# One state product for two chunks: 104-column chunks in the scan of a delta-rule attention kernel

## The chip, the cores and the metric

The kernel runs on one NeuronCore of one Trainium2 chip. The metric is the device time of one execution in microseconds (us); the time of a kernel is the median of several executions.

## The reference

What is computed first is a linear recurrence with a 40 x 40 state for each of 4 x 8 heads, over 768 steps; then a mixture of experts is applied to its output (8 experts, each token goes to one of them or is passed through).

```python
def _attn_ref(r, k, v, w, a, b):          # each [4, 8, 768, 40]
    state = zeros((B, H, D, D))
    for t in range(S):
        y[:, :, t] = einsum('bhd,bhde->bhe', rt, state)
        Sa = einsum('bhde,bhe->bhd', state, at)
        state = state * wt[:, :, None, :] - einsum('bhd,bhe->bhde', Sa, bt)
        state = state + einsum('bhd,bhe->bhde', vt, kt)
def reference(...): x = attn_out as [3072, 320]; return _moe_ref(x, w_skip, w_gate, w1, w2)
```

## The kernel before

**Chunks.** The 768 steps are cut into 24 chunks of 32 steps (`c`), and the 32 heads into two sides (`x` = 0, 1) of 16 heads (`u`). Two chunks make a pair, `c//2`: decays, masks and the inverse triangular matrices are made for a pair, and four chunks share one triangular inversion. For each side a tile `R1[x][c%2]`, 128 partitions x 16 heads x 72 columns, stands for a chunk. Its columns 0 to 39 are the transposed state with the decay of the pair; its columns 40 to 71 are one column for each of the 32 queries `r` of the chunk. Its partitions hold 40 rows of state, 32 rows of `v`, and 32 rows of solved terms `U`.

**The steps of one chunk and side**, with the engines and lines:

- `rs` (L288): 16 products of the state `SS[x]` with `r`, 32 columns each; two copies into columns 40 to 71 of the state rows. In an even chunk the copies are on VectorE and multiply by a decay `Dx` (L292), in an odd chunk they are plain ScalarE copies (L293).
- `m2` (L207, L209): 16 products of `v` and `r`, 32 columns; four ScalarE copies into the rows of `v`. It runs one chunk ahead.
- `ux` (L302, L304): 16 products of `R1` with the keys, 72 columns; one ScalarE copy into `UXs`.
- `uq` (L313, L315, L317): 16 products with the inverse triangle, 72 columns; four ScalarE copies into the `U` rows; a mask multiply over the 32 query columns on GpSimd.
- `sst` (L325, L330): the new state, twice. 16 products give it transposed (`ST`), copied into columns 0 to 39 of the next chunk's `R1` (L335 on ScalarE after an even chunk, L334 on VectorE with the decay of the next pair after an odd one); 16 more with the operands exchanged give it untransposed (`S2`), copied into `SS` (L338), which only `rs` reads.
- `yy` (L348, L352): 16 products of the query columns give the output.

Every matmul of these steps is fp32 and appears in the trace as two TensorE instructions, so that 16 products are a group of 32.

**The order of the work** is written out by hand for TensorE, ScalarE and VectorE: each issues in the order of the program text. One turn of the chunk loop runs `rs(c,0)`, `uq(c-1,1)`, `yy(c-1,0)`, `ux(c,0)`, `sst(c-1,1)`, `m2(c+1,0)`, `uq(c,0)`, `rs(c,1)`, `yy(c-1,1)`, `sst(c,0)`, `ux(c,1)`, `m2(c+1,1)`. Between them stand pieces of other work: `m1` (L163 to L174, products of the keys), `kbt` (L185, L188) and `wtt` (L197, L199), which are transposes; `route` (L628 to L684), which transposes the finished output, picks an expert and scatters tokens; scans of the decays (L114, L126); and the generator `T()`, one step of the triangular inversion on VectorE (L228, L230). GpSimd's order alone is set by a scheduler. With four chunks per inversion, a turn of the loop comes in four kinds, `j = c%4`: scans stand in the even turns (`j` = 0 and 2), transposes `kbt` in the odd ones.

**Loads.** `load_rv` brings `r` and `v` of a chunk as one tile (L104), issued from GpSimd's queue at the end of a turn, two chunks ahead into two buffers; its buffer is free when `rs` and `m2` of the older chunk are done.

After the loop come the experts (L729 to L797), some 150 us that read nothing of the above but the tokens.

Of the kernel before, what the change touches and what calls it, by code (L numbers as in the profile page):

```python
# [57 lines left out]
def attn(ctx,tc,i,m,out,X):  # L58
# [43 lines left out]
    def load_rv(c,E=G):  # L102
        if c>=NC: return
        rvt[c]=wk2.tile([128,2,16,32],F32,tag="rvt",name="rvt"); E.dma_start(rvt[c],i['rv'][c])  # L104
# [95 lines left out]
    def m2(c,x):  # L200
        if c>=NC: return
        t=rvt[c]; rr=t[:,0].rearrange("p (b h) t -> p b h t",b=2); vv=t[:,1].rearrange("p (b h) t -> p b h t",b=2)
        Pp=ps_p.tile([128,4,32],F32,tag="pp",name="psP")
        for hh in range(4):
            for b in (0,2,1,3):
                s=slice(64*(b//2),64*(b//2)+40)
                TE.matmul(Pp[32*b:32*b+32,hh,:],vv[s,b%2,2*hh+x,:],rr[s,b%2,2*hh+x,:],start=True,stop=True)  # L207
        for b in range(4):
            A.copy(R1[x][c%NR1][ao[x]:ao[x]+32,4*b:4*b+4,40:72],Pp[32*b:32*b+32])  # L209
# [70 lines left out]
    def rs(c,x):  # L280
        if c>=NC: return
        cc=c%2; rr=rvt[c][:,0].rearrange("p (b h) t -> p b h t",b=2)
        R=R1[x][c%NR1]; e=slice(eo[x],eo[x]+40)
        RS=ps_c.tile([128,8,32],F32,tag="pc",name="psRS")
        for hh in range(4):
            for b in (0,2,1,3):
                s=slice(64*(b//2),64*(b//2)+40); v=(b%2)*4+hh
                TE.matmul(RS[s,v,:],SS[x][:,b//2,v,:],rr[:,b%2,2*hh+x,:],start=True,stop=True)  # L288
        for bh in range(2):
            s=slice(64*bh,64*bh+40)  # L290
            o=R[e,8*bh:8*bh+8,40:72]
            if cc==0: V.tensor_tensor(o,RS[s],H[c//2]['Dx'][x][s].unsqueeze(2).broadcast_to([40,8,32]),ALU.mult)  # L292
            else: A.copy(o,RS[s])  # L293
    UXd={}
    def ux(c,x):
        if c>=NC: return
        R=R1[x][c%NR1]; l1=L1[x][(c//2)%NL]
        UX=ps_c.tile([128,4,72],F32,tag="pc",name="psUX")
        for hh in range(4):
            for b in range(4):  # L300
                u=4*b+hh
                TE.matmul(UX[32*b:32*b+32,hh,:],l1[:,u,c%2,:],R[:,u,:],start=True,stop=True)  # L302
        UXs=wk2.tile([128,4,72],F32,tag="UX",name="UXs")
        A.copy(UXs,UX)  # L304
        UXd[x]=UXs
    def uq(c,x):
        if c<0: return
        R=R1[x][c%NR1]; Tb=TBa[(c//2)%NTB]; uu=slice(uo[x],uo[x]+32)
        UQ=ps_c.tile([128,4,72],F32,tag="pc",name="psUQ")
        for hh in range(4):  # L310
            for b in range(4):
                q=slice(32*b,32*b+32)
                TE.matmul(UQ[q,hh,:],Tb[q,x*8+hh*2+c%2,:],UXd[x][q,hh,:],start=True,stop=True)  # L313
        for b in range(4):
            A.copy(R[uu,4*b:4*b+4,:],UQ[32*b:32*b+32,:,:])  # L315
# [1 line left out]
        (V if c==NC-1 else G).tensor_tensor(R[pq,:,40:72],R[pq,:,40:72],mQ[pq].unsqueeze(1).broadcast_to([64,16,32]),ALU.mult)  # L317
    def sst(c,x):
        if c<0 or c+1>=NC: return
        R=R1[x][c%NR1]; Rn=R1[x][(c+1)%NR1]; l2=L2[x][(c//2)%NL2]; cc=c%2; e=slice(eo[x],eo[x]+40)  # L320
        ST=ps_s.tile([128,8,40],F32,tag="ps",name="psST")
        for hh in range(4):
            for b in (0,2,1,3):
                u=4*b+hh; v=(b%2)*4+hh; s=slice(64*(b//2),64*(b//2)+40)
                TE.matmul(ST[s,v,:],l2[:,cc,u,:],R[:,u,0:40],start=True,stop=True)  # L325
        S2=ps_s.tile([128,8,40],F32,tag="ps",name="psS")
        for hh in range(4):
            for b in (0,2,1,3):
                u=4*b+hh; v=(b%2)*4+hh; s=slice(64*(b//2),64*(b//2)+40)
                TE.matmul(S2[s,v,:],R[:,u,0:40],l2[:,cc,u,:],start=True,stop=True)  # L330
        for bh in range(2):
            s=slice(64*bh,64*bh+40)
            o=Rn[e,8*bh:8*bh+8,0:40]
            if cc==1: V.tensor_tensor(o,ST[s],H[c//2+1]['Dx'][x][s].unsqueeze(2).broadcast_to([40,8,40]),ALU.mult)  # L334
# [5 lines left out]
    def yy(c,x):  # L340
# [4 lines left out]
        for hh in range(4):  # L345
            for b in range(4):
                u=4*b+hh
                TE.matmul(Y[32*b:32*b+32,2*hh+x,:],R[:,u,40:72],l2[:,cc,u,:],start=True,stop=True)  # L348
# [556 lines left out]
```

## Time and profile before

| | |
|---|---|
| median of 3 runs | 662.38 us (660.09 to 664.48) |
| the profiled execution's own time | 663.83 us |
| its span, first to last instruction | 662.1 us |
| loop over chunks, about | 66 us to 510 us |
| mean granted TensorE clock | 0.888 |
| VectorE / ScalarE / GpSimd busy | 489.7 / 419.5 / 324.2 us |

The rows that follow come from one profiled execution. A row of the groups gives line, engine, operation, tiles, shape and count, then busy time and mean duration of one, then the idle time before it. A row of the chain gives start, length and what ran: the chain follows the last instruction back to what released it, each time, or to its predecessor on its engine. A row of the timeline gives start, length, instructions merged into it, and in brackets the idle time ahead. "issue" in the place of a releaser is a wait for which the trace shows no cause. `PEld` is TensorE's weight load.

### The profile page before, as it was taken

What the parts mean: (1) busy time and instruction counts of PE and PEld (TensorE: products, weight loads), DVE (VectorE), ACT (ScalarE), POOL (GpSimd) and SP (SyncE); (2) the same over time, 40 slices, a digit from 0 to 9 for tenths busy, and PEclk for the clock granted to TensorE, in tenths of its full rate; (3) what the DMA queues carried; (4) which work ended last, traced back from release to release, by engine and by line L of the source; (5) the groups of instructions that cost most, each with busy time, mean ns of one, the idle gap of its engine ahead of it and who ended that gap; (6) DMA issues with size and microseconds to landing.
All of it is one profiled execution on the core that took longest, in us unless ns stands there. A gap on an engine that the chain in (4) does not pass through costs nothing.

```text
span 662.1 us, 33508 instructions
## 1 busy us (share of the span) xinstructions
PE 515.5 (78%) x14772; PEld 432.2 (65%) x14772; DVE 489.7 (74%) x1182; ACT 419.5 (63%) x1151; POOL 324.2 (49%) x246
## 2 busy tenths in 40 slices
PE   4777776676776787767785877878886899999995
PEld 1543456565664576656664666666775599999995
DVE  7998697858997479973999736864166457888881
ACT  5463674586965778567785677887885354555540
POOL 5481951648545375553946442223132155666661
PEclk8786895799977898878889689988788999999998
DMA  7473665352443525335253333453365266676210
GB/s 227 152 242 107 166 207 160 104 177 63 139 125 107 174 63 150 109 112 168 83 156 88 107 113 81 140 153 113 105 178 167 73 183 201 214 229 216 77 48 24
DMA packets 67446, 91.06 MB, mean 138 GB/s; under 512 B 32564, under 2 KB 54657, under 8 KB 65806
## 3 DMA queue, kind: packets, MB, share of 16 engines
q1 hardware_dynamic: 62350, 74.05, 38.1%
q0 software_dynamic: 4944, 14.80, 6.6%
q8 instruction: 118, 1.93, 1.2%
q14 instruction: 34, 0.28, 0.1%
HBM read 74.03 MB, written 17.08 MB: 138 GB/s over the span
## 4 chain that ended last, share of the span: by engine, by line
PE 24%; DVE 11%; ACT 8%; issue 5%; DMA 2%; POOL 1%; SPq 0%; POOLq 0%; DVEq 0%; ACTq 0%
PE pc L782 5%; PE ps L793 4%; PE px L782 3%; ACT R1t L315 2%; PE py L793 2%; ACT L2t L188 2%; DVE M L228 2%; PE ps L325 2%; DVE ti L789 2%; PE pc L313 1%; PE pc L288 1%; DVE M L230 1%; PE ps L330 1%; ACT SS L338 1%; ACT R1t L209 1%
## 5 line engine op out<-in xcount | busy, mean ns | idle before, releaser
L317 POOL TENSOR_TENSOR R1t<-R1t,mc 64x512 f32<-64x512 f32 x46 | 60.5, 1315 | 104.7 <-ACT R1t L315 72.6
L315 ACT COPY R1t<-pc 32x288 f32<-32x288 f32 x192 | 74.9, 390 | 20.7 <-PE pc L313 17.6
L730 POOL TENSOR_TENSOR WL<-WR,WH 128x1280 fp32r<-128x1280 f32 (+1 forms) x21 | 57.7, 2782 | 8.7 <-ACT WH L729 8.6
L188 ACT COPY L2t<-pq 64x160 f32<-64x160 f32 x184 | 52.8, 287 | 7.5 <-PE pq L185 5.1
L684 POOL DMA_INDIRECT xg<-XS,ix x24 | 25.5, 1064 | 64.3 <-DMA xg<-XS,ix 26.0
L325 PE MATMUL ps<-R1t,L2t 128*40 128x40 f32 x1472 | 48.2, 221 | 11.0 <-issue 5.3
L143 POOL TENSOR_TENSOR WR<-WR,M 128x1024 f32<-128x1024 f32 (+1 forms) x19 | 44.2, 2332 | 25.8 <-DVE M L114 19.7
L228 DVE TENSOR_TENSOR M<-M 128x22 f32<-128x22 f32 (+10 forms) x110 | 55.0, 500 | 0.0
L325 PEld LDWEIGHTS ps<-R1t,L2t 128*40 128x40 f32 x1472 | 39.3, 132 | 18.9 <-ACT R1t L315 8.9
L338 ACT COPY SS<-ps 40x320 f32<-40x320 f32 x92 | 38.7, 420 | 19.9 <-PE ps L330 18.5
L209 ACT COPY R1t<-pq 32x128 f32<-32x128 f32 x184 | 47.2, 256 | 5.5 <-PE pq L207 1.3
L288 PE MATMUL pc<-rvt,SS 128*40 128x32 f32 x1472 | 44.9, 216 | 7.2 <-issue 4.8
L288 PEld LDWEIGHTS pc<-rvt,SS 128*40 128x40 f32 x1472 | 38.3, 135 | 15.4 <-issue 7.8
L330 PE MATMUL ps<-L2t,R1t 128*40 128x40 f32 x1472 | 42.9, 218 | 6.5 <-issue 6.4
L313 PE MATMUL pc<-UXs,TB 32*32 32x72 f32 x1536 | 43.1, 255 | 6.0 <-issue 5.9
L330 PEld LDWEIGHTS ps<-L2t,R1t 128*40 128x40 f32 x1472 | 38.2, 134 | 7.3 <-issue 7.2
L230 DVE TENSOR_TENSOR M<-M 128x22 f32<-128x22 f32 (+10 forms) x110 | 40.8, 371 | 0.0
L230 DVE TENSOR_TENSOR px<-px,M 128x168 f32<-128x168 f32 (+8 forms) x150 | 39.1, 260 | 1.4
L729 ACT CAST WH<-WR 128x1024 fp32r<-128x1024 f32 (+1 forms) x35 | 39.6, 1132 | 0.0
L313 PEld LDWEIGHTS pc<-UXs,TB 32*32 32x32 f32 x1536 | 32.1, 122 | 11.4 <-issue 8.9
L789 DVE CAST ti<-xe 128x2 int32<-128x2 f32 x8 | 39.3, 4911 | 0.2
L174 DVE STREAM_TRANSPOSE M<-pq 128x128 f32<-128x128 f32 x40 | 12.1, 308 | 36.9 <-ACT M L165 24.3
(240 smaller groups left out, 1529.3 us busy)
## 6 DMA issues: line engine op xcount, KB each, us to landing
rvt<-rv POOLq DMA_DIRECT2D x21, 512.0 KB, 3.9
WR<-kb SPq DMA_DIRECT2D x10, 1024.0 KB
WR<-w SPq DMA_DIRECT2D x16, 640.0 KB
WR<-w SPq DMA_DIRECT2D x16, 512.0 KB
M<-wt SPq DMA_DIRECT2D x9, 520.5 KB
M<-at SPq DMA_DIRECT2D x8, 512.0 KB
WR<-w SPq DMA_DIRECT2D x16, 256.0 KB
R1t<-vt SPq DMA_DIRECT2D x48, 80.0 KB
```

Source lines behind the costliest of these rows:

```text
L188: A.copy(L2[x][h%NL2][64-64*x:128-64*x,c,bb*4:bb*4+4,:],pt[64*c:64*c+64,:,64*x:64*x+40])
L209: A.copy(R1[x][c%NR1][ao[x]:ao[x]+32,4*b:4*b+4,40:72],Pp[32*b:32*b+32])
L228: V.tensor_tensor(tv,NLt[:,j,j+1:32].unsqueeze(2).broadcast_to([128,n,k]),X[:,j,lo:hi].unsqueeze(1).broadcast_to([128,n,k]),ALU.mult)
L230: for tv,xv in q: V.tensor_tensor(xv,xv,tv,ALU.subtract)
L288: TE.matmul(RS[s,v,:],SS[x][:,b//2,v,:],rr[:,b%2,2*hh+x,:],start=True,stop=True)
L313: TE.matmul(UQ[q,hh,:],Tb[q,x*8+hh*2+c%2,:],UXd[x][q,hh,:],start=True,stop=True)
L315: A.copy(R[uu,4*b:4*b+4,:],UQ[32*b:32*b+32,:,:])
L317: (V if c==NC-1 else G).tensor_tensor(R[pq,:,40:72],R[pq,:,40:72],mQ[pq].unsqueeze(1).broadcast_to([64,16,32]),ALU.mult)
L325: TE.matmul(ST[s,v,:],l2[:,cc,u,:],R[:,u,0:40],start=True,stop=True)
L330: TE.matmul(S2[s,v,:],R[:,u,0:40],l2[:,cc,u,:],start=True,stop=True)
L730: def low(s,E,o,x,h): E.tensor_tensor(s.R(o),x,h,ALU.subtract)
L782: for n,(a,b) in enumerate(mm): TE.matmul(ph[:,g],R(a),R(b),start=n==0,stop=n==7)
```

## The change

An even chunk's `R1` gets 104 columns: 40 of state, 32 with the queries of the *next* (odd) chunk, 32 with its own. `rs` of an even chunk multiplies the state with both chunks' queries (64 columns), and `m2` and the steps after it carry the extra 32 columns along. `sst` of an even chunk then applies its keys to 72 columns at once: out come the transposed state and, beside it, that state times the odd chunk's queries, which are just the 72 columns that the odd chunk's `R1` needs. So an odd chunk has no `rs`, and an even chunk makes no `S2` and no copy into `SS`. The mask is needed for an even chunk's own 32 columns alone. `r` is laid out by pairs on the host (tile `rrt`, own columns second) and `v` by chunks (`vvt`); GpSimd issues a load of `vvt` in each turn and one of `rrt` in each odd turn.

```diff
+        rrt[h]=wk2.tile([128,16,64],F32,tag="rrt",name="rrt"); E.dma_start(rrt[h],i['rr'][h])
     def m2(c,x):
+        n=(64,32)[c%2]
-        Pp=ps_p.tile([128,4,32],F32,tag="pp",name="psP")
+        Pp=ps_p.tile([128,4,n],F32,tag="pp",name="psP")
...
     def rs(c,x):
-        if c>=NC: return
+        if c>=NC or c%2: return
-        RS=ps_c.tile([128,8,32],F32,tag="pc",name="psRS")
+        RS=ps_c.tile([128,8,64],F32,tag="pc",name="psRS")
...
-            if cc==0: V.tensor_tensor(o,RS[s],H[c//2]['Dx'][x][s].unsqueeze(2).broadcast_to([40,8,32]),ALU.mult)
-            else: A.copy(o,RS[s])
+            V.tensor_tensor(R[e,8*bh:8*bh+8,40:104],RS[s],H[c//2]['Dx'][x][s].unsqueeze(2).broadcast_to([40,8,64]),ALU.mult)
     def ux(c,x):
+        R=R1[x][c%NR1]; l1=L1[x][(c//2)%NL]; n=RW[c%2]
-        UX=ps_c.tile([128,4,72],F32,tag="pc",name="psUX")
+        UX=ps_c.tile([128,4,n],F32,tag="pc",name="psUX")
...
     def sst(c,x):
+        if cc==0:
+            for hh in range(4):
+                for b in (0,2,1,3):
+                    u=4*b+hh; s=slice(64*(b//2),64*(b//2)+40)
+                    TE.matmul(P2[s,b%2,72*hh:72*hh+72],l2[:,0,u,:],R[:,u,0:72],start=True,stop=True)
+            for bh in range(2):
+                A.copy(Rn[e,8*bh:8*bh+8,:].rearrange("p (b h) n -> p b (h n)",b=2),P2[64*bh:64*bh+40,:,0:288])
+            return
...
             load_rv(c+2,G if c else SP)
+            if c%2 or c==0: load_rr((c+3)//2,G if c else SP)
```

`RW` is (104, 72); `uq` takes its width from it in the same way.
`P2` joins the two PSUM banks that `ST` and `S2` used in turn.

The first place is ScalarE in an odd turn with `j` = 3, from the copies of `sst(c-1,1)` to those of `sst(c,0)`. Before:

```order
L335 COPY R1t<-ps_102 40x8x40 x2
L338 COPY SS_117<-ps_101 40x320 x2
L647 ACTIVATE ex<-sb 128x16
L209 COPY R1t<-pq_104 32x4x32 x4
L315 COPY R1t<-pc_99 32x288 x4
L293 COPY R1t<-pc_100 40x8x32 x2
L188 COPY L2t<-pq_105 64x160 x4
L232 COPY M<-px_106 128x32x8
L338 COPY SS_116<-ps_101 40x320 x2
```

The same stretch now, where all lines have moved down by some ten:

```order
L334 COPY R1t<-ps 40x576 x2
L661 ACTIVATE ex<-sb 128x16
L217 COPY R1t<-pq_102 32x4x64 x4
L322 COPY R1t<-pc_100 32x288 x4
L195 COPY L2t<-pq_103 64x160 x4
L240 COPY M<-px_104 128x32x8
L351 COPY SS_115<-ps 40x320 x2
```

The two copies into `SS` of the even chunk and the two of the odd chunk's `rs` are gone; the copies of `sst` grew from 320 to 576 elements per partition and those of `m2` from 128 to 256.

The second place is TensorE, in the same kind of turn, from its start. Before:

```order
L288 MATMUL pc_100<-rvt,SS_116 40x32 x16
L313 MATMUL pc_99<-UXs,TB 32x72 x16
L185 MATMUL pq_105<-mc,WR 128x104 x4
L348 MATMUL py_103<-L2t,R1t 32x40 x16
L636 MATMUL pq_104<-wg,xT 32x9 x12
L302 MATMUL pc_100<-R1t,L1t 32x72 x16
L185 MATMUL pq_105<-mc,WR 128x104 x4
L325 MATMUL ps_102<-R1t,L2t 40x40 x16
L330 MATMUL ps_101<-L2t,R1t 40x40 x16
```

And now:

```order
L320 MATMUL pc_100<-UXs,TB 32x104 x16
L192 MATMUL pq_103<-mc,WR 128x104 x4
L361 MATMUL py_101<-L2t,R1t 32x40 x16
L650 MATMUL pq_102<-wg,xT 32x9 x12
L309 MATMUL pc_99<-R1t,L1t 32x72 x16
L192 MATMUL pq_103<-mc,WR 128x104 x4
L332 MATMUL ps<-R1t,L2t 40x72 x16
```

The product with `r` at the head of the turn and the second state product are gone; `uq` of the even chunk's side 1 has 104 columns and its state product 72.

The third place is GpSimd, whose order the scheduler made anew, in an even turn with `j` = 2. Before:

```order
L684 DMA xg<-XS,ix 2048x322 x2
L170 TENSOR_TENSOR M<-M,mc 128x256
L143 TENSOR_TENSOR WR<-WR,M 128x32x32
L317 TENSOR_TENSOR R1t<-R1t,mc 64x16x32
L132 COPY D_3446<-D 40x8 x2
L132 COPY D_3449<-D 40x8 x2
L143 TENSOR_TENSOR WR<-WR,M 128x32x32
```

And now:

```order
L698 DMA xg<-XS,ix 2048x322
L324 TENSOR_TENSOR R1t<-R1t,mc 64x16x32
L698 DMA xg<-XS,ix 2048x322
L177 TENSOR_TENSOR M<-M,mc 128x256
L150 TENSOR_TENSOR WR<-WR,M 128x32x32
L139 COPY D_3239<-D 40x8 x2
L139 COPY D_3242<-D 40x8 x2
L324 TENSOR_TENSOR R1t<-R1t,mc 64x16x32
L150 TENSOR_TENSOR WR<-WR,M 128x32x32
```

One mask multiply (L317, now L324) now stands between the two scatters of `route`, and the mask of this turn behind the four copies of decays instead of ahead of them.

Over the whole program TensorE has 768 fewer of its matmuls (1536 fewer instructions in the trace's count), ScalarE 96 fewer copies, and GpSimd 10 more issues of a DMA.

More of the change, by code (lines that the diff above doesn't have):

```diff
@@ L63, in attn @@
     pp=m.pp
-    ps_c,ps_s,ps_y,ps_p,ps_x=(Ring(pp,n,k) for n,k in (("pc",2),("ps",2),("py",1),("pq",2),("px",1))); m.ps=ps_p
+    ps_c,ps_s,ps_y,ps_p,ps_x=(Ring(pp,n,k) for n,k in (("pc",2),("ps",0),("py",1),("pq",2),("px",1))); m.ps=ps_p
+    P2=pp.tile([128,2,512],F32,name="ps"); ps_s.t=[P2[:,q] for q in range(2)]
     V,A,G,TE,SP=nc.vector,nc.scalar,nc.gpsimd,nc.tensor,nc.sync
@@ L83, in attn @@
     TBa=[TB[:,512*q:512*q+512].rearrange("p (h m) -> p h m",h=16) for q in range(NTB)]
-    L2t=cp.tile([128,5120],F32,name="L2t"); R1t=cp.tile([128,4608],F32,name="R1t")
+    L2t=cp.tile([128,5120],F32,name="L2t"); R1t=cp.tile([128,5632],F32,name="R1t")
     L2=[[L2t[:,1280*(2*n+x):1280*(2*n+x)+1280].rearrange("p (c u d) -> p c u d",c=2,u=16) for n in range(NL2)] for x in range(2)]
-    R1=[[R1t[:,1152*(2*n+x):1152*(2*n+x)+1152].rearrange("p (u n) -> p u n",u=16) for n in range(NR1)] for x in range(2)]
+    R1=[[R1t[:,3328*n+(1664,1152)[n]*x:][:,:(1664,1152)[n]].rearrange("p (u n) -> p u n",u=16) for n in range(NR1)] for x in range(2)]
+    RW=(104,72)
     SS=[cp.tile([128,2,8,40],F32,name=f"SS{x}") for x in range(2)]
@@ L103, in load_rv, with load_rr @@
         if c>=NC: return
-        rvt[c]=wk2.tile([128,2,16,32],F32,tag="rvt",name="rvt"); E.dma_start(rvt[c],i['rv'][c])
+        rvt[c]=wk2.tile([128,16,32],F32,tag="vvt",name="vvt"); E.dma_start(rvt[c],i['vv'][c])
+    rrt={}
+    def load_rr(h,E=G):
+        if h>=NH: return
+        rrt[h]=wk2.tile([128,16,64],F32,tag="rrt",name="rrt"); E.dma_start(rrt[h],i['rr'][h])
     def load_v(c,x):
@@ L201, in m2 @@
         if c>=NC: return
-        t=rvt[c]; rr=t[:,0].rearrange("p (b h) t -> p b h t",b=2); vv=t[:,1].rearrange("p (b h) t -> p b h t",b=2)
-        Pp=ps_p.tile([128,4,32],F32,tag="pp",name="psP")
+        n=(64,32)[c%2]
+        rr=rrt[c//2][:,:,0:n].rearrange("p (b h) t -> p b h t",b=2); vv=rvt[c].rearrange("p (b h) t -> p b h t",b=2)
+        Pp=ps_p.tile([128,4,n],F32,tag="pp",name="psP")
         for hh in range(4):
@@ L208, in m2 @@
         for b in range(4):
-            A.copy(R1[x][c%NR1][ao[x]:ao[x]+32,4*b:4*b+4,40:72],Pp[32*b:32*b+32])
+            A.copy(R1[x][c%NR1][ao[x]:ao[x]+32,4*b:4*b+4,40:40+n],Pp[32*b:32*b+32])
     def tinv(ph):
@@ L280, in rs @@
     def rs(c,x):
-        if c>=NC: return
-        cc=c%2; rr=rvt[c][:,0].rearrange("p (b h) t -> p b h t",b=2)
+        if c>=NC or c%2: return
+        rr=rrt[c//2].rearrange("p (b h) t -> p b h t",b=2)
         R=R1[x][c%NR1]; e=slice(eo[x],eo[x]+40)
-        RS=ps_c.tile([128,8,32],F32,tag="pc",name="psRS")
+        RS=ps_c.tile([128,8,64],F32,tag="pc",name="psRS")
         for hh in range(4):
@@ L302, in ux @@
                 TE.matmul(UX[32*b:32*b+32,hh,:],l1[:,u,c%2,:],R[:,u,:],start=True,stop=True)
-        UXs=wk2.tile([128,4,72],F32,tag="UX",name="UXs")
-        A.copy(UXs,UX)
+        UXs=wk2.tile([128,4,104],F32,tag="UX",name="UXs")
+        A.copy(UXs[:,:,0:n],UX)
         UXd[x]=UXs
@@ L324, in sst @@
                 u=4*b+hh; v=(b%2)*4+hh; s=slice(64*(b//2),64*(b//2)+40)
-                TE.matmul(ST[s,v,:],l2[:,cc,u,:],R[:,u,0:40],start=True,stop=True)
+                TE.matmul(ST[s,v,:],l2[:,1,u,:],R[:,u,0:40],start=True,stop=True)
         S2=ps_s.tile([128,8,40],F32,tag="ps",name="psS")
@@ L329, in sst @@
                 u=4*b+hh; v=(b%2)*4+hh; s=slice(64*(b//2),64*(b//2)+40)
-                TE.matmul(S2[s,v,:],R[:,u,0:40],l2[:,cc,u,:],start=True,stop=True)
+                TE.matmul(S2[s,v,:],R[:,u,0:40],l2[:,1,u,:],start=True,stop=True)
         for bh in range(2):
             s=slice(64*bh,64*bh+40)
-            o=Rn[e,8*bh:8*bh+8,0:40]
-            if cc==1: V.tensor_tensor(o,ST[s],H[c//2+1]['Dx'][x][s].unsqueeze(2).broadcast_to([40,8,40]),ALU.mult)
-            else: A.copy(o,ST[s])
+            V.tensor_tensor(Rn[e,8*bh:8*bh+8,0:40],ST[s],H[c//2+1]['Dx'][x][s].unsqueeze(2).broadcast_to([40,8,40]),ALU.mult)
         for bh in range(2):
@@ L347, in yy @@
                 u=4*b+hh
-                TE.matmul(Y[32*b:32*b+32,2*hh+x,:],R[:,u,40:72],l2[:,cc,u,:],start=True,stop=True)
+                TE.matmul(Y[32*b:32*b+32,2*hh+x,:],R[:,u,RW[cc]-32:RW[cc]],l2[:,cc,u,:],start=True,stop=True)
         if x==1:
```

16 lines of the change are left out of this document (7 added, 9 removed).

## The prediction

> **What bounds the kernel now.** I read the page first, for the shares of the engines, and its DMA part for one queue.
>
> ```profile
> PE 515.5 (78%) x14772; PEld 432.2 (65%) x14772; DVE 489.7 (74%) x1182; ACT 419.5 (63%) x1151; POOL 324.2 (49%) x246
> ...
> q8 instruction: 118, 1.93, 1.2%
> ```
>
> No engine is full over the span, so the shares say little. The stages say more. This is the view by windows, cut at the turns of the loop: the stretch from 324 to 369 us is an odd turn and the even turn behind it (chunks 13 and 14), 369 to 387 is the odd turn of chunk 15, 387 to 405 the even turn of chunk 16.
>
> ```profile
> core 0: us, PE busy (x) PEld busy (x) DVE busy (x) ACT busy (x) POOL busy (x), PEclk, DMA share, GB/s
> 324.00:369.00 45.00, 31.81 (x1183) 26.31 (x1184) 44.04 (x134) 30.66 (x93) 26.77 (x24) 0.87 0.41 119
> 369.00:387.00 18.00, 15.25 (x515) 12.33 (x517) 10.11 (x32) 15.32 (x47) 8.09 (x6) 0.85 0.49 150
> 387.00:405.00 18.00, 14.29 (x613) 12.00 (x614) 6.72 (x21) 12.32 (x38) 6.63 (x7) 0.91 0.30 85
> 405.00:510.00 105.00, 83.56 (x3189) 70.60 (x3189) 63.07 (x220) 82.46 (x251) 28.18 (x25) 0.89 0.47 138
> ```
>
> The first three rows, 45, 18 and 18 us, are one round of four turns, 81 us. Two of its turns belong to VectorE: 44.04 of 45 us busy, with the inversion and the scans. Only then do ScalarE and TensorE take turns. The chain of waits says the same, and where our operations stand in it:
>
> ```profile
> 324.50 0.43 DVE R1t L292
> ...
> 348.74 0.42 DVE R1t L292
> ...
> 364.41 0.44 DVE R1t L292
> ...
> 368.83 0.90 PE pq L628 x3
> 369.74 1.21 PE pc L288 x32
> 370.95 1.16 PE pc L313 x32
> ...
> 396.26 1.18 issue
> ```
>
> The copies of the even chunks' `rs` (L292) head and stand in VectorE's stretch. The odd chunk's `rs` (L288 at 369.74) heads the stretch that follows, and ScalarE carries it on, back to back:
>
> ```profile
> 377.68 0.86 ACT L338 COPY SS<-ps 40x320 f32<-40x320 f32 x2
> ...
> 378.81 1.06 ACT L209 COPY R1t<-pq 32x128 f32<-32x128 f32 x4
> 379.89 1.62 ACT L315 COPY R1t<-pc 32x288 f32<-32x288 f32 x4
> 381.53 0.76 ACT L293 COPY R1t<-pc 40x256 f32<-40x256 f32 x2
> ```
>
> The last row of the chain above is a stall of TensorE in the middle of a group. The timeline shows how it comes:
>
> ```profile
> 392.17 0.71 PE L302 MATMUL pc<-R1t,WR 128*32 128x72 f32 x32
> 392.69 0.63 PE L163 MATMUL pq<-WR,L1t 128*32 128x64 f32 x32
> 393.25 0.81 PE L325 MATMUL ps<-R1t,L2t 128*40 128x40 f32 x32
> 393.89 0.79 PE L330 MATMUL ps<-L2t,R1t 128*40 128x40 f32 x32
> 394.61 0.46 PE L636 MATMUL pq<-wg,xT 128*32 128x9 f32 x20
> ...
> 397.44 0.55 PE L163 MATMUL pq<-WR,L1t 128*32 128x64 f32 x25 [1.18 <-issue]
> 397.92 0.80 PE L288 MATMUL pc<-rvt,SS 128*40 128x32 f32 x32
> 398.66 0.49 PE L348 MATMUL py<-L2t,R1t 128*32 128x40 f32 x32
> 399.08 0.81 PE L325 MATMUL ps<-R1t,L2t 128*40 128x40 f32 x32
> 399.72 0.32 PE L330 MATMUL ps<-L2t,R1t 128*40 128x40 f32 x7
> 401.29 0.69 PE L330 MATMUL ps<-L2t,R1t 128*40 128x40 f32 x25 [1.25 <-issue]
> ```
>
> From one stall to the next stand 25+32+32+32+7 = 128 matmuls, each with its weight load: 256 instructions. All of TensorE's 29,544 divided by 256 is 115, and the instruction queue moved 118 packets. So TensorE runs out of fetched instructions wherever it gets through 128 matmuls too fast, here in 2.6 us (397.44 to 400.04). The Trainium skill (Runtime: NRT & Kernel Launch, section Instruction fetch mechanics) has the blocks of 256 instructions too, but says that fetching is mostly hidden behind issue; the trace does not agree, with 1.18 and 1.25 us lost in two blocks running.
>
> **The change part by part.** The prices come from these groups, by form:
>
> ```profile
> L315 ACT COPY R1t<-pc 32x288 f32<-32x288 f32 x192 | 74.9, 390 | 20.7 <-PE pc L313 17.6
> ...
> L209 ACT COPY R1t<-pq 32x128 f32<-32x128 f32 x184 | 47.2, 256 | 5.5 <-PE pq L207 1.3 <-POOL R1t L317 1.0 <-issue 0.9
> ...
> L338 ACT COPY SS<-ps 40x320 f32<-40x320 f32 x92 | 38.7, 420 | 19.9 <-PE ps L330 18.5
> ...
> L334 DVE TENSOR_TENSOR R1t<-ps,D 40x320 f32<-40x320 f32 x44 | 21.3, 484 | 8.5 <-PE ps L325 7.9
> ...
> L292 DVE TENSOR_TENSOR R1t<-pc,D 40x256 f32<-40x256 f32 x44 | 18.5, 421 | 3.7 <-PE pc L288 2.8
> ...
> L104 POOL DMA_DIRECT2D rvt<-rv x21 | 12.8, 612 | 45.3 <-PE pc L288 45.3
> ```
>
> *ScalarE.* From 128 to 288 elements a copy grows from 256 to 390 ns, 0.84 ns for each element. So 320 to 576 elements cost 0.21 us more, 128 more elements 0.11 us. For a pair and side it loses the copies into `SS` (0.86) and those of the odd `rs` (0.76), and gains 2 x 0.21 in `sst`, 4 x 0.11 in `uq`, 4 x 0.11 in `m2`, 0.11 in `ux`: 1.62 less against 1.41 more. Its work does not change, it moves.
>
> *VectorE.* From 256 to 320 elements its multiply grows from 421 to 484 ns, 0.98 ns for each; 512 elements cost 0.25 us more. All 44 together are 11 us more, and nothing leaves this engine.
>
> *TensorE.* For a pair and side go `S2` (393.89 to 394.61, 0.72 us) and the odd `rs` (397.92 to 398.66, 0.74). Five groups get wider, and the trace has none of these widths. For the even `rs`, 32 to 64 columns, the bounds are 0 (at 32 columns it takes 0.74, `ST` with 40 takes 0.64, so width does not show) and 0.74 (in proportion). The nearest rows are `yy` with 40 columns (0.42) and `m1` with 64 (0.56), a third more for 24 columns; I take 0.3. For `ST`, 40 to 72, 0 to 0.5, by the same rows 0.25; for `ux` (72 columns, 0.52) and `uq` 0 to 0.25 each, 0.2; for `m2`, 0 to 0.4, 0.14. That is 1.46 less and about 1.1 more, with 0 and 2.1 as ends.
>
> *GpSimd.* Ten more issues at 0.61 us; the 45.3 us that it waited for `rs` before issuing a load end, since the new buffers come free a turn earlier. What stood behind that wait were masks that wait for ScalarE anyway. I take nothing.
>
> *What lies on the path*, for one round of four turns (81 us):
>
> VectorE's stretch and the scans ahead of it hold three calls of the even `rs`, two copies each: 3 x 2 x 0.25 = +1.5 us, with 0 as the other end if VectorE had slack; at 98% busy it has none. That the odd turn inside it has shorter work on TensorE and ScalarE buys nothing there: both wait for VectorE.
>
> In the odd turn from 369 us the first `rs` goes (-1.21), and `uq`, which runs slow here (1.16), gets wider (+0.3). On ScalarE -0.86 (L338) and -0.76 (L293), +0.43 each in `uq`, `sst` and `m2`: -0.3. Together -1.2 us, between -0.5 and -2.
>
> The even turn from 387 us is TensorE's: two `rs` (+0.6), `ux`, `uq` and `ST` (+0.65) against `S2` (-0.72); `SS` (-0.86) against +0.43. That would be -0.1; the wider groups stand between stalls, where a longer block only shortens the wait for the next, so it could be -1.2. As fetching gets a term of its own, I take 0, to +1.2 if the stalls lie elsewhere.
>
> The sum of a round is +0.3 us, or 5.5 rounds from 66 to 510 us: +1.6, between -18 and +12 by the ends just named. The start, with wider first `m2` and `ux` and larger clears: +0.5. Fetching: 1536 fewer matmuls are 12 fewer blocks. The two stalls shown lie in one stretch that the chain runs through; elsewhere it stands on VectorE or ScalarE, and a block costs nothing. I put a third of the 12 on the path, at 1.2 us: -4 (0 to -14). The Trainium skill's section named above would make this term nothing, and the sum 665.9 where the next line has 661.9.
>
> The profiled execution took 663.83 us; +1.6 +0.5 -4 gives 661.9. It lay 1.45 us above the median of the runs, so I forecast **660.5 us**.
>
> **The rivals.**
>
> *The odd turns pay in full.* The chain between two chunks loses two round trips (state to ScalarE to `rs` to ScalarE to `ux`) in every odd turn. If each of the eleven gained the 1.2 us of chunk 15 and the wide groups of the even turns hid behind other work, and half the fetches were on the path (-7), it would be 663.8 - 13 - 7, less 1.45 for the median: about 643. For it: in the last 100 us VectorE is not the bound (63 of 105). Against it: of every four turns, 45 us are VectorE's.
>
> *VectorE's wider copies decide, and the time is longer.* In 66 to 510 us every even turn has a scan or the inversion ahead of L292; if all 44 copies are paid (+11) and the odd turns give nothing back because VectorE is late there too, it is 663.8 + 11 - 1.45 = 673. It decides from the point where what an odd turn gains (1.2) is less than two calls cost (1.0) plus what comes of it. For it: 44.04 of 45 us. Against it: from 369 us on VectorE is half idle.
>
> *GpSimd's new order.* The mask of an even turn now stands behind four copies of decays; if `yy` waits for it, TensorE stands still. The copies from 361.45 to 364.4 cost 2.9 us in a place, five times: +14, 676.
>
> ```profile
> 360.11 1.28 POOL L317 TENSOR_TENSOR R1t<-R1t,mc 64x512 f32<-64x512 f32 x1
> 361.45 2.92 POOL L132 COPY D<-D 40x8 f32<-40x8 f32 x4
> ```
>
> Against it: this `yy` belongs to the next turn and stands behind its `uq`, which runs at 370.95 in the chain above; 364.4 is early enough.
>
> **How the numbers follow.** A measurement of this kernel tells about 1%, 6.6 us. The forecast's case (gains and costs cancel) has 0.42, with 653 to 668 as its own range; the odd turns in full 0.30, VectorE 0.19, GpSimd's order 0.09. The second case gives faster by over 1%, and a little of the first (0.07) does; the last two give slower, except for a few hundredths where they are paid in part. So faster 0.36, within 1% 0.38, slower 0.26. The range of 8 in 10 reaches into the cases on both sides: 643 to 675.
>
> **What would show it.** Right: in the profile after, `sst`'s copies of 576 elements take about 0.63 us, VectorE's of 512 about 0.67, the group of `rs` about 1.0 us; VectorE is still at 95% and more in the odd turn after its inversion begins and the even one behind it; the ScalarE-bound odd turn is about 1 us shorter, the even turn not; the instruction queue moves some 106 packets. Wrong: if the VectorE-bound turns themselves get shorter, then VectorE was kept busy by contention and not by its own work; if TensorE's wide groups cost nothing, or twice what I took, the even turns show it first; if `yy` waits for GpSimd's mask, its order decided.

## The result, and the profile after

The changed kernel takes **708.16 us** (median of 4 runs, 707.4 to 710.5), beside 663.43 us of the kernel before on the same chip: a ratio of **1.0685, 95% interval 1.0632 to 1.0739**. It is slower by 45 us. The prediction, 660.5 us with a range of 643 to 675, was wrong, and on the wrong side. The medians given here are of all executions; a ratio and its interval leave out the few slow ones (1 of 4 of the join alone, 3 of 10 and 1 of 8 of the change without the join) and are not the quotient of the medians.

The profiled execution took 708.75 us, its span is 706.9 us where the one before was 662.1. The page first, as in the prediction:

```profile
PE 543.9 (77%) x13236; PEld 450.1 (64%) x13236; DVE 475.6 (67%) x1182; ACT 416.5 (59%) x1055; POOL 323.2 (46%) x256
...
q8 instruction: 106, 1.74, 1.0%
```

Nobody has more to do: VectorE and ScalarE are busy for less time than before (489.7 and 419.5 us), GpSimd for as long, and TensorE, though it has 1536 instructions fewer, shows 28 us more. 45 us more with no more work on the other engines suggests waits. The view by windows says where. These are the windows of the kernel before, cut within 0.6 us of the head of `route`'s transposes in an odd turn (325.5), in the next odd turn (368.8) and the one behind (403.8), and at the start of the last copy of `ux` (516.0), where the loop is taken to end:

```profile
core 0: us, PE busy (x) PEld busy (x) DVE busy (x) ACT busy (x) POOL busy (x), PEclk, DMA share, GB/s
325.50:368.80 43.30, 30.81 (x1159) 25.48 (x1150) 42.44 (x128) 30.66 (x93) 25.27 (x21) 0.87 0.41 120
368.80:403.80 35.00, 29.01 (x1119) 24.11 (x1119) 15.87 (x54) 26.48 (x80) 14.13 (x12) 0.87 0.39 119
403.80:516.00 112.20, 88.89 (x3335) 74.89 (x3336) 65.48 (x224) 86.78 (x264) 29.87 (x27) 0.88 0.45 132
516.00:662.10 146.10, 135.18 (x1158) 128.59 (x1156) 102.91 (x146) 64.72 (x96) 75.36 (x39) 0.98 0.46 143
```

The same four pieces of the program in the kernel after:

```profile
337.00:383.00 46.00, 31.98 (x1034) 25.71 (x1024) 43.03 (x128) 29.39 (x81) 23.95 (x22) 0.85 0.35 104
383.00:422.00 39.00, 33.32 (x982) 27.49 (x986) 16.84 (x55) 26.69 (x75) 14.65 (x14) 0.74 0.36 100
422.00:541.00 119.00, 91.36 (x2885) 73.95 (x2870) 66.87 (x221) 85.16 (x234) 29.32 (x29) 0.86 0.42 121
541.00:706.90 165.90, 142.26 (x1158) 134.89 (x1158) 89.14 (x149) 64.82 (x97) 76.63 (x40) 0.93 0.43 126
```

The loop ends 25 us later (541 against 516), a little in each turn. The surprise is the last row: the experts behind the loop, where the change edits not one line, take 165.9 us instead of 146.1. The waits name both places. A row gives who waited, for whom, and the sum, count and longest of it in us. Before, of the copies into `SS`, of `ST`'s copies, and of the experts' first product:

```profile
ACT hH L783 <- PE pc L782: 38.4, 21, 6.3
...
ACT SS L338 <- PE ps L330: 18.5, 22, 3.7
...
DVE R1t L334 <- PE ps L325: 7.9, 4, 4.1
```

After:

```profile
ACT hH L797 <- PE pc L796: 54.2, 21, 13.3
ACT SS L351 <- DVE R1t L348: 43.5, 18, 5.7
...
DVE R1t L348 <- PE ps L345: 15.2, 14, 3.4
...
PEld ps L807 <- DVE ro L810: 12.3, 3, 5.7
...
PE ps L807 <- DVE ro L810: 11.5, 3, 5.5
```

Three releasers are new. ScalarE's copy of `S2` into `SS` (L351) waits for VectorE's copy of the *other* product, `ST` (L348), 43.5 us in all; VectorE's copy of `ST` waits for `S2` (L345), which it doesn't read; and behind the loop, the experts' second product (L807) waits for VectorE's read of its predecessor (L810). The two rows of L807 are the same three waits, seen once at TensorE's weight loads and once at its products, so 12 us in all and not 24. No data flows along any of the three. The program's own list of waits has them too. A copy of `S2` waited for TensorE alone, and now waits for VectorE as well (DVE is VectorE, PE TensorE):

```
before  L338 COPY SS_116<-ps_101 40x320 [waits PE_49]
after   L351 COPY SS_115<-ps 40x320 [waits DVE_49,PE_49]
```

The timeline of the kernel after shows one such wait in an odd turn. The rows are TensorE's two products, then VectorE, then ScalarE:

```profile
310.81 1.51 PE L340 MATMUL ps<-R1t,L2t 128*40 128x40 f32 x29 [0.55 <-ACT R1t L322]
...
312.12 1.33 PE L345 MATMUL ps<-L2t,R1t 128*40 128x40 f32 x31
...
312.81 1.99 DVE L243 STREAM_TRANSPOSE TB<-M 128x1024 f32<-128x1024 f32 x1 [2.97 <-ACT M L240]
314.65 0.97 DVE L348 TENSOR_TENSOR R1t<-ps,D 40x320 f32<-40x320 f32 x2
...
312.40 0.37 ACT L240 COPY M<-px 128x256 f32<-128x256 f32 x1
315.71 0.85 ACT L351 COPY SS<-ps 40x320 f32<-40x320 f32 x2 [2.93 <-DVE R1t L348]
```

`S2` is ready at 313.45 us (312.12 + 1.33) and ScalarE is free at 312.77. But it stands still until 315.6, when VectorE, which had a transposition of 2 us in hand, has copied `ST`; everything queued behind L351 on ScalarE stands still with it. Before, the two copies could run side by side, here VectorE's at 178.95 and ScalarE's at 179.00:

```profile
178.95 0.98 DVE L334 TENSOR_TENSOR R1t<-ps,D 40x320 f32<-40x320 f32 x2
...
179.00 0.85 ACT L338 COPY SS<-ps 40x320 f32<-40x320 f32 x2
```

Of VectorE's 44 copies of `ST`, 17 overlapped with a copy into `SS` before (in 13 of 22 places), and none after. The Trainium skill (PSUM — Partial Sum Buffer, section Specifications (TRN2)) says that ScalarE and VectorE can use PSUM in parallel as long as their banks differ; the trace of before agrees, with both copies at full speed side by side (0.85 us for two here, 2 x 0.42 in the groups). So the chip did not ask for the new wait.

**The theory** (J in the expectations): the two PSUM banks of the ring `ps_s`, from which `ST`, `S2` and behind the loop one of the experts' products take their buffers, are now two halves of one tile `P2`. Waits are made by tile. Whoever takes one half waits for all that was done with the other.

### The profile page after: what moved, and what is told of

Same layout as the page of the kernel before. It is cut to its first block, busy times and chain, and to the rows that moved or that the text cites. A ratio compares the mean times of both kernels' runs of the same rounds, so it can differ in the third digit from the quotient of the medians.

```text
span 706.9 us, 30312 instructions
## 1 busy us (share of the span) xinstructions
PE 543.9 (77%) x13236; PEld 450.1 (64%) x13236; DVE 475.6 (67%) x1182; ACT 416.5 (59%) x1055; POOL 323.2 (46%) x256
## 5 line engine op out<-in xcount | busy, mean ns | idle before, releaser
L324 POOL TENSOR_TENSOR R1t<-R1t,mc 64x512 f32<-64x512 f32 x46 | 60.8, 1322 | 147.2 <-ACT R1t L322 128.1
L322 ACT COPY R1t<-pc 32x416 f32<-32x416 f32 (+1 forms) x192 | 85.2, 444 | 21.0 <-PE pc L320 17.5
L217 ACT COPY R1t<-pq 32x256 f32<-32x256 f32 (+1 forms) x184 | 57.5, 312 | 4.2 <-issue 0.8
L320 PE MATMUL pc<-UXs,TB 32*32 32x72 f32 (+1 forms) x1536 | 48.5, 273 | 3.7 <-issue 3.2
L215 PE MATMUL pq<-rrt,vvt 40*32 40x64 f32 (+1 forms) x1472 | 33.3, 238 | 22.4 <-ACT L2t L195 18.5
L351 ACT COPY SS<-ps 40x320 f32<-40x320 f32 x44 | 18.5, 420 | 53.8 <-DVE R1t L348 43.5
L215 PEld LDWEIGHTS pq<-rrt,vvt 40*32 40x32 f32 x1472 | 25.5, 128 | 29.7 <-ACT L2t L195 20.9
L311 ACT COPY UXs<-pc 128x416 f32<-128x416 f32 (+1 forms) x48 | 21.8, 454 | 35.5 <-PE pc L309 33.6
L332 PE MATMUL ps<-R1t,L2t 128*40 128x72 f32 x768 | 38.6, 254 | 4.2 <-ACT R1t L322 4.1
L340 PE MATMUL ps<-R1t,L2t 128*40 128x40 f32 x704 | 27.0, 231 | 18.5 <-ACT R1t L322 15.6
L807 PE MATMUL ps<-WH,hH 128*128 128x320 f32 x88 | 29.9, 340 | 11.5 <-DVE ro L810 11.5
```

Of the source, the lines that this page charges most:

```text
L217: A.copy(R1[x][c%NR1][ao[x]:ao[x]+32,4*b:4*b+4,40:40+n],Pp[32*b:32*b+32])
L320: TE.matmul(UQ[q,hh,:],Tb[q,x*8+hh*2+c%2,:],UXd[x][q,hh,0:n],start=True,stop=True)
L324: (V if c==NC-1 else G).tensor_tensor(o,o,mQ[pq].unsqueeze(1).broadcast_to([64,16,32]),ALU.mult)
L807: for n,(a,b) in enumerate(mm): TE.matmul(po,R(a),R(b),start=n==0,stop=n==23)
```

## The experiments

### The join alone, in the kernel before

```diff
-    ps_c,ps_s,...=(Ring(pp,n,k) for n,k in (("pc",2),("ps",2),("py",1),("pq",2),("px",1)))
+    ps_c,ps_s,...=(Ring(pp,n,k) for n,k in (("pc",2),("ps",0),("py",1),("pq",2),("px",1)))
+    P2=pp.tile([128,2,512],F32,name="ps"); ps_s.t=[P2[:,q] for q in range(2)]
```

> The kernel before, with one thing from the change: the two PSUM banks of the state products are one tile of two halves; no group is wider and none is removed. Theory J (the joined tile brings waits between its halves): the stage behind the loop, the same code in all kernels, grows from 146 to about 166 us, with TensorE waiting some 24 us in it for VectorE's read of the other half; in the odd turns ScalarE's copy into SS waits for VectorE's copy of the transposed state, some 20 us more in the loop; 695 to 708 us in all. Theory W (the wider groups and VectorE's wider copies cost the time): nothing changes, 663 us.

Measured: 701.04 us (694.41 to 705.51), ratio 1.0496 (1.0412 to 1.058). Two lines that neither compute nor move anything cost the kernel before 5%. Its loop ends at 539.1 instead of 516.0 us, and the experts take 160.4 instead of 146.1. Its waits have the same rows under its own line numbers:

```profile
ACT hH L784 <- PE pc L783: 53.9, 21, 14.0
...
ACT SS L339 <- DVE R1t L335: 36.6, 19, 2.9
...
DVE R1t L335 <- PE ps L331: 15.2, 12, 4.9
...
PEld ps L794 <- DVE ro L797: 12.0, 3, 5.4
```

### The change without the join

```diff
-    P2=pp.tile([128,2,512],F32,name="ps"); ps_s.t=[P2[:,q] for q in range(2)]
...
+            Pk=[ps_s.tile([128,4,72],F32,tag="ps",name="psK") for _ in range(2)]
-                    TE.matmul(P2[s,b%2,72*hh:72*hh+72],l2[:,0,u,:],R[:,u,0:72],start=True,stop=True)
+                    TE.matmul(Pk[b%2][s,hh,:],l2[:,0,u,:],R[:,u,0:72],start=True,stop=True)
-                A.copy(Rn[e,8*bh:8*bh+8,:].rearrange("p (b h) n -> p b (h n)",b=2),P2[64*bh:64*bh+40,:,0:288])
+                for k in range(2):
+                    A.copy(Rn[e,8*bh+4*k:8*bh+4*k+4,:],Pk[k][64*bh:64*bh+40])
```

The ring has its two banks as separate tiles again. The even state product fills both; four copies of 288 elements take the place of two of 576. All else is the change, but for ScalarE's time: the four copies of `sst` take 33.0 us in all where the two took 30.4.

> The changed kernel with the two banks as two tiles again; the copies of an even chunk's state are four of 288 elements instead of two of 576, which is some 0.3 us more of ScalarE for each even chunk and side, 7 us in all, part of it on the path. Theory J: the stage behind the loop is back at 146 us, no copy into SS waits for VectorE, 660 to 672 us. Theory W: the wider groups are all there, so at least 695 us.

> The kernel of e2 again, on the chip of these three, as their measure and for a profile: 661 to 670 us, the loop of the same length as before within 5 us, 146 us behind it, no copy into SS that waits for VectorE.

Measured: 667.35 us, ratio 1.0028 (0.9989 to 1.0066), and in another series 668.85 us, ratio 1.0045 (1.001 to 1.0081). Without the join the change gains nothing, and may lose 2 or 3 us. I call it the split kernel. The rows that were new are gone, and those of the kernel before are back:

```profile
ACT hH L798 <- PE pc L797: 38.1, 21, 6.5
...
ACT SS L352 <- PE ps L346: 18.8, 20, 3.7
```

### The two places of the join, one at a time

Behind the loop: the experts' second product gets one half of `P2` and the bank of `ps_y`, no longer both halves; its ring has two buffers where it had three.

```diff
-        m.pr=[Ring.of(ps_c.t+ps_x.t),Ring.of(ps_s.t+ps_y.t),ps_p]
+        m.pr=[Ring.of(ps_c.t+ps_x.t),Ring.of(ps_s.t[:1]+ps_y.t),ps_p]
```

> The changed kernel; only the ring of PSUM banks for the experts' second product holds one half of the joined tile and another bank, no longer both halves. Theory J: the stage behind the loop goes from 166 back to about 146 us, the loop stays as it is, 688 us. Theory W: nothing changes, 708 us.

In the loop: the odd `S2` gets a bank of the ring `ps_c`, so `ST` has `P2` to itself.

```diff
-        S2=ps_s.tile([128,8,40],F32,tag="ps",name="psS")
+        S2=ps_c.tile([128,8,40],F32,tag="pc",name="psS")
```

> The changed kernel; only the untransposed state of an odd chunk is made in another PSUM ring (the one that the odd chunk's product with r used before), so that it shares no tile with the transposed state. Theory J: the waits of the copy into SS for VectorE (43.5 us) go and VectorE's copy no longer waits for the second product (15.2 us); the loop gets 15 to 25 us shorter, the stage behind it keeps its 166 us: 683 to 693 us. Theory W: within 1% of 708 us.

Measured, one run each: 695.23 and 683.54 us. The windows of the first, loop and experts:

```profile
66.00:542.70 476.70, 361.41 (x11124) 292.71 (x11124) 329.30 (x952) 317.18 (x880) 213.07 (x191) 0.80 0.42 121
542.70:693.50 150.80, 138.78 (x1158) 131.20 (x1158) 99.83 (x149) 64.69 (x96) 75.96 (x40) 0.95 0.45 139
```

And of the second:

```profile
66.00:516.20 450.20, 337.03 (x11124) 273.55 (x11124) 332.73 (x952) 317.51 (x879) 214.94 (x191) 0.85 0.45 129
516.20:681.80 165.60, 142.62 (x1158) 135.02 (x1158) 89.72 (x149) 64.72 (x96) 76.34 (x40) 0.92 0.41 126
```

Each mends its own place and leaves the other as it was. The experts go from 165.8 to 150.8 us (15.0 less; the loop after ends at 541.1), and the loop's end from 541.1 to 516.2 (24.9 less), which is where it was before. Together that is 39.9 us of the 44.8 us of span that were lost; the split kernel, which mends both, has 39.4 less (706.9 and 667.5). Of the 5.4 us that it keeps, 4.0 lie in the experts (150.1 us against 146.1).

### Why nothing is gained when the join is gone

The change removes `S2` and its copies after every even chunk and `rs` and its copies from every odd one. Is that worth nothing, or does something take it back? This kernel is the one before with only the removal: nothing becomes wider, and the odd chunk's query columns get no state. (`SS` is still made after each odd chunk, so an even chunk's `rs` has the right state, which the text below denies.)

```diff
     def rs(c,x):
-        if c>=NC: return
+        if c>=NC or c%2: return
...
-        S2=ps_s.tile([128,8,40],F32,tag="ps",name="psS")
+        if cc:
+            S2=ps_s.tile([128,8,40],F32,tag="ps",name="psS")
...
+        if cc==0: return
```

> The kernel before, without the work that the change removes and with no group wider: an odd chunk has no product with r and no copies of it, an even chunk no second state product and no copies into SS, so that odd chunks' outputs lack their state and even ones use an old one. Theory B (the removal does shorten the odd turns, by 1.2 us or more each, and the wider groups of the even turns take it back): 10 to 25 us below the kernel before. Theory H (the removed work was hidden behind VectorE anyway): less than 5 us below it.

Measured: 647.68 us (646.44 to 648.28), ratio 0.9738 (0.971 to 0.9767). The removal is worth 17.5 us, and the wider steps take all of it back. Cut as the windows above, its profile shows where:

```profile
318.60:362.50 43.90, 28.44 (x994) 22.93 (x990) 43.11 (x128) 27.37 (x85) 25.21 (x22) 0.80 0.39 114
362.50:395.10 32.60, 25.34 (x991) 20.82 (x991) 16.24 (x54) 23.26 (x71) 13.51 (x11) 0.90 0.45 128
395.10:494.00 98.90, 77.64 (x2858) 63.69 (x2853) 64.86 (x223) 75.69 (x234) 28.22 (x26) 0.86 0.52 149
494.00:645.60 151.60, 138.22 (x1158) 131.30 (x1158) 96.10 (x148) 64.80 (x96) 76.28 (x40) 0.95 0.47 138
```

The loop ends 22 us earlier than before, and 13.3 of them come from its last stretch (98.9 us where it took 112.2); VectorE's two turns are no shorter (43.9 and 43.3). The experts are 5.5 us longer. Which of the wider steps take it back? First VectorE's copies of the even `rs` in the split kernel, of which this kernel makes only the chunk's own 32 columns:

```diff
-            V.tensor_tensor(R[e,8*bh:8*bh+8,40:104],RS[s],H[c//2]['Dx'][x][s]...broadcast_to([40,8,64]),ALU.mult)
+            V.tensor_tensor(R[e,8*bh:8*bh+8,72:104],RS[s][:,:,32:64],H[c//2]['Dx'][x][s]...broadcast_to([40,8,32]),ALU.mult)
```

> The kernel with the split banks (e2); VectorE's copies of an even chunk's product with r take the chunk's own 32 columns alone, 256 elements as before; the 32 columns for the next chunk are not written, so that the odd chunks' outputs lack their state. Theory V (VectorE's stretch sets two turns of four, and the 44 wider copies, 0.27 us more each, are what the change still costs there): 6 to 11 us below e2. Theory P (TensorE's and ScalarE's wider groups are the cost): within 3 us of e2.

Measured: 665.89 us, ratio 1.0028 (0.9999 to 1.0057), beside 1.0045 of the split kernel in the same series. By the ratios that is 1 us, by the medians 3, and the intervals overlap: VectorE's wider copies alone are not it.

Then the products against ScalarE's copies. The first of these two keeps the wide products and makes the copies narrow, VectorE's as above and ScalarE's like this:

```diff
-            A.copy(R1[x][c%NR1][ao[x]:ao[x]+32,4*b:4*b+4,40:40+n],Pp[32*b:32*b+32])
+            A.copy(R1[x][c%NR1][ao[x]:ao[x]+32,4*b:4*b+4,40+n-32:40+n],Pp[32*b:32*b+32,:,n-32:n])
-            A.copy(R[uu,4*b:4*b+4,:],UQ[32*b:32*b+32,:,:])
+            A.copy(R[uu,4*b:4*b+4,0:72],UQ[32*b:32*b+32,:,0:72])
-                    A.copy(Rn[e,8*bh+4*k:8*bh+4*k+4,:],Pk[k][64*bh:64*bh+40])
+                    A.copy(Rn[e,8*bh+4*k:8*bh+4*k+4,0:40],Pk[k][64*bh:64*bh+40,:,0:40])
```

> The change with two separate bank tiles (the split kernel, 667 to 669 us), in which the wide products stay and their results are copied narrow. Even chunks: the copies of `rs` and `m2` take only the chunk's own 32 columns, those of `uq` 72 instead of 104 columns, those of the state 40 instead of 72; the one copy of `ux` stays. So the columns of the odd chunk's queries are left out, and the own query columns lack their solved terms; the states are right. Removing alone was worth 17.5 us, and widening took about 20 back. Theory T, the products: what is taken back is time of TensorE's wider groups (1.6 us more for a pair and side by their pitch); then this kernel gains no more than VectorE's narrow copy did, and takes 660 to 667 us. Rival A, the copies: each of ScalarE's copies lies in the chain from product to product, and 1.3 us of them for a pair and side go; then 645 to 655 us. If both count, 655 to 660.

The second makes the products narrow and keeps the copies as wide as they are, which read a part of the narrow result twice:

```diff
-                TE.matmul(RS[s,v,:],SS[x][:,b//2,v,:],rr[:,b%2,2*hh+x,:],start=True,stop=True)
+                TE.matmul(RS[s,v,:],SS[x][:,b//2,v,:],rr[:,b%2,2*hh+x,32:64],start=True,stop=True)
-                TE.matmul(UX[32*b:32*b+32,hh,:],l1[:,u,c%2,:],R[:,u,:],start=True,stop=True)
+                TE.matmul(UX[32*b:32*b+32,hh,:],l1[:,u,c%2,:],R[:,u,0:72],start=True,stop=True)
...
-            A.copy(R[uu,4*b:4*b+4,:],UQ[32*b:32*b+32,:,:])
+            if c%2: A.copy(R[uu,4*b:4*b+4,:],UQ[32*b:32*b+32,:,:])
+            else: A.copy(R[uu,4*b:4*b+4,:].rearrange('p h (k n) -> p h k n',k=2),UQ[32*b:32*b+32,:,0:52].unsqueeze(2).broadcast_to([32,4,2,52]))
```

> The split kernel again, the other way round: the copies stay as wide as in the change (they read 32 or 52 columns twice), but the products of `rs`, `m2`, `ux` and `uq` of even chunks have the width that they had before; only the state product keeps 72 columns. The odd chunk's query columns and the output are not computed rightly, the states are. Theory T: 1.1 of the 1.6 us for a pair and side go, and the time falls to 650 to 657 us. Rival A: the copies decide and it stays at 664 to 670 us. If both count, 657 to 664.

Measured: narrow copies 647.3 us, ratio 0.9748 (0.9675 to 0.9822); narrow products 668.73 us, ratio 1.0054 (1.0009 to 1.0098). The theory of the products falls in both. One row of the page for each kernel shows it best. The split kernel, narrow products, narrow copies, and the removal alone:

```profile
PE 522.9 (78%) x13236; PEld 433.9 (65%) x13236; DVE 491.5 (74%) x1182; ACT 419.2 (63%) x1103; POOL 322.5 (48%) x256
```

```profile
PE 506.2 (76%) x13236; PEld 420.7 (64%) x13236; DVE 489.1 (74%) x1182; ACT 418.5 (63%) x1103; POOL 324.4 (49%) x256
```

```profile
PE 511.5 (79%) x13236; PEld 422.8 (66%) x13236; DVE 484.9 (75%) x1182; ACT 388.0 (60%) x1103; POOL 335.5 (52%) x256
```

```profile
PE 486.1 (75%) x13236; PEld 405.6 (63%) x13236; DVE 483.3 (75%) x1182; ACT 382.6 (59%) x1055; POOL 320.6 (50%) x246
```

The first two differ by 17 us of TensorE's time and take the same time, though the second had a lower granted clock (0.849 against 0.864); so do the last two, with 25 us between them. What goes with the time is the copies: ScalarE is busy for 419 us at a ratio of 1.005, twice, and for 388 and 383 us at 0.975 and 0.974. The narrow copies include VectorE's (484.9 us against 491.5). Those alone gave little, but no kernel here has all of ScalarE's narrow and VectorE's wide, so that ScalarE's share of the 20 us isn't shown.

### Does it matter where on ScalarE?

Two parts of the narrow copies by themselves: those of `m2`, which run a chunk ahead, and those of `uq` and the state, which stand in the chain from one product to the next. The edits are the first line of the diff of the narrow copies, and its other two.

> The split kernel (1.0045 of the time before), in which only the copies of `m2` of even chunks are narrow, 128 elements instead of 256: the queries' columns of the odd chunk are left out in the rows of `v`. 96 copies by 0.11 us are 10 us less of ScalarE's time, in a step that runs a chunk ahead and has nobody waiting for it at once. All copies narrow gave 31 us less of ScalarE's time and 20 us less of the kernel's. Theory O: it is ScalarE's time that counts, wherever it lies, since the chain comes by behind whatever stands ahead in its queue; then 6 to 7 us less, a ratio of 0.993 to 0.996. Rival L: it is the length of the chain from product to copy to product; `m2` isn't in it, and the ratio stays at 1.002 to 1.007.

> The split kernel, in which only the copies of `uq` (288 elements instead of 416) and of the state (160 instead of 288) of even chunks are narrow; the odd chunk's query columns and the solved terms of the own ones are left out. 96 copies by 0.11 us and 96 by 0.11 us are 21 us less of ScalarE's time, all of it in the chain from product to copy to product. Theory O: two thirds of that, 13 to 14 us less, a ratio of 0.983 to 0.986. Rival L: all that narrow copies gave comes from here, 18 to 20 us, a ratio of 0.974 to 0.978.

Measured: 664.55 us, ratio 0.9989 (0.9956 to 1.0022), and 662.51 us, ratio 0.9954 (0.9913 to 0.9995), with 409 and 398 us of ScalarE. Neither theory meets both. Against the split kernel's 1.0045, `m2` gives 0.006, more than the rival allowed and less than the theory asked, with an interval that reaches both; the copies in the chain give 0.009, half of the lower forecast and outside both. With VectorE's 0.002 the parts come to 0.016, and all at once give 0.030. So the parts seem to be worth more together than alone; the difference, 0.013, is hardly more than its error, some 0.012 by the intervals. It would fit several engines which bound the turns in alternation, so that one gains little until the next is relieved too; that was not tried and stays open.

### A version that puts copies on VectorE

In the last chunks VectorE is the least busy of the three (65 of 112 us in the window quoted), so half of the even state copies of the split kernel went there from chunk 16 on.

```diff
-                    A.copy(Rn[e,8*bh+4*k:8*bh+4*k+4,:],Pk[k][64*bh:64*bh+40])
+                    (V.tensor_copy if c>15 and k else A.copy)(Rn[e,8*bh+4*k:8*bh+4*k+4,:],Pk[k][64*bh:64*bh+40])
```

> e2, with one of the two copies of each half of an even chunk's state on VectorE from chunk 16 on, where the inversions have ended and VectorE is half idle while ScalarE runs back to back. If ScalarE sets these last turns: 2 to 5 us below e2, 660 to 663 us. If not: the same as e2.

Measured: 672.51 us, ratio 1.0112 (1.0056 to 1.0168): a miss, slower than the split kernel. VectorE issues in the order of the program, and here it stood still four times until the state product came, the longest for 9.0 us:

```profile
DVE R1t L335 <- PE ps L332: 17.1, 4, 9.0
```

Its own work behind that copy waited as long; that this is what made the kernel slower is likely, but not shown. No kernel tried here that does all of the work beats the one before.

## Why the prediction was wrong, point by point

**The step that failed** is one that isn't there. The part on the change has no term for the joining of the two banks: the description of the change names it (`P2` joins the two PSUM banks), and the sum goes on to prices of instructions. "Its work does not change, it moves" is true of ScalarE, 419.5 us before and 416.5 after, but its waits changed: 43.5 us for VectorE at L351. And the experts were set aside as reading "nothing of the above but the tokens", though one of their products takes its buffers from the ring that was joined. Those two places are 24.9 and 15 of the 44.8 us. They were to be seen ahead of the run: the waits of the changed program name VectorE at every first copy into `SS`, and the experts' ring is a line of the kernel.

**The rest of the forecast** can be judged on the split kernel, which is the change without that step but for the 2.6 us more of ScalarE's copies.

- *The sizes* were right for the copies: 634 ns for those of 576 elements (0.63 forecast), 687 for VectorE's of 512 (0.67), 497 against 390 for `uq` (0.11 more). Of the products, the state product was the term that was too small. From the start of a group to the start of the next, where the granted clock was 1.00, `rs` took 1.02 us (1.04 forecast), `uq` and `ux` 0.85 after 0.63 and 0.64 (0.2 more forecast), `m2` 0.58 (0.53), but the state product 1.13 (0.89). Before, `rs` took 0.74 us, the state product 0.64 and `m2` 0.39. Where the clock was 0.50 the state product took 2.08 us in the split kernel. The 1.21 us of the odd `rs` at 369.74 were at 0.50 too; the `rs` at 397.92, at 1.00, took 0.74. None of this width cost anything that could be measured: the narrow products show it for `rs`, `m2`, `ux` and `uq`, and the narrow copies beside the removal alone for the state product as well.
- *The sums* have slips. The groups priced at 393.89 (`S2`) and 397.92 (`rs`) belong to an odd and an even chunk, and so to those that stay; they have the shape of those that go. The even turn's terms, +0.6, +0.65, -0.72, -0.86 and +0.43, come to +0.1 and not to -0.1, and they count one `ux` where the turn has two of an even chunk. The turn was taken as 0 all the same. A third of 12 blocks at 1.2 us is 4.8 and not 4, which moves the forecast by less than 1 us.
- *The two turns of VectorE* were to be 1.5 us longer. Cut as above they go from 43.3 to 44.7 us in the split kernel, 1.4 more:

```profile
331.50:376.20 44.70, 31.26 (x1022) 25.56 (x1018) 41.21 (x127) 30.33 (x88) 22.07 (x20) 0.84 0.35 100
376.20:411.00 34.80, 28.16 (x991) 23.02 (x991) 17.34 (x55) 26.52 (x77) 13.87 (x12) 0.90 0.41 112
411.00:517.40 106.40, 83.88 (x2853) 68.71 (x2853) 64.93 (x221) 85.44 (x249) 31.15 (x29) 0.90 0.47 135
517.40:667.50 150.10, 137.83 (x1158) 130.43 (x1158) 101.28 (x149) 64.69 (x96) 75.31 (x39) 0.96 0.46 140
```

  The size fits, the reason less: VectorE is busy for 92% of them and not for 95% or more, and its narrow copies gave back only 1 to 3 us in the whole kernel. Such single profiles carry an error: executions of one kernel differ by several us (664.1 to 670.6 for the split kernel).
- *One round times 5.5.* The forecast carried one round over the whole loop, but the last stretch isn't such a round. It took 112.2 us before and takes 106.4 in the split kernel, 5.8 less, and what lies ahead of it loses that again: the first cut moved from 325.5 to 331.5 us. The removal alone gained most there too. So the sum without its term for fetching came out at the time of the split kernel by errors that cancel, which is luck.
- *The odd turn on ScalarE and the even one behind it* were to be 1.2 us shorter together. They are 0.2 us shorter (35.0 and 34.8); in the kernel after they are 4 us longer. The 1.2 us came mostly from TensorE (-1.21 for `rs`). The removal alone does make these two turns 2.4 us shorter (32.6), so the wider steps take it back here too. ScalarE's own sum in that turn, -0.3, came nearer.
- *Fetching*: 106 packets, as forecast, but the gain of 4 us does not show. The sum with the other terms alone would be 663.8 + 1.6 + 0.5, less 1.45 for the median: 664.5 us, a ratio of 1.003 to 662.38; the split kernel has 1.0028 and 1.0045. The Trainium skill's rule (Runtime: NRT & Kernel Launch, section Instruction fetch mechanics: the cost of a block is mostly hidden) would have made this term nothing, and these sums agree with it, though an error in another term could do the same.
- *The rivals.* "The odd turns pay in full" (643 us) comes near what the removal is worth by itself (647.68 us), though more than half of that lies in the last stretch and not evenly in eleven odd turns; the wider copies take it back. "VectorE's wider copies decide" (673 us) has 1 to 3 us to show. "GpSimd's new order" doesn't show: in the trace of the split kernel and of the kernel after, `yy` never waits for GpSimd. None of them had the wait that decided, since all three were made from the work that moves and none from what a buffer's owner waits for.

**What stays open**: the 4 us that the split kernel loses behind the loop, where TensorE is busy for 137.8 us at a granted clock of 0.96 and before for 135.2 at 0.98. The kernel with only the removal, which has no wider group, loses 5.5 us there at 0.95, so it isn't the width. Open are also the split of the copies' 20 us between ScalarE and VectorE, and which engine takes over when one of ScalarE's copies is made shorter alone.

## What to carry to other kernels

Where a change makes one tile of two buffers, list everyone who uses either half, in every stage that shares them, and ask of each whom it will now wait for; here this cost 37 us in the kernel before and 39 in the changed one, with no instruction of the engines more. When steps are merged, price the copies behind the products first: here the copies' extra columns, ScalarE's and VectorE's together, cost 20 us, and those of the products nothing that could be measured. A removal and what it widens should be run apart, since their sum, near nothing, hid 17 us and more of each.
